# Scaling w_down by gb on chip, one VectorE step per output piece, and a last tile in finer pieces

## The chip, the cores and the metric

The kernel runs on one core of a Trainium2 chip. The metric is the device time of one execution in microseconds (us). A profile shows the span from the first to the last instruction; the time is 1.9 to 2.0 us longer than the span. TensorE (PE; its weight loads are listed as PEld) multiplies matrices and accumulates in PSUM, of which the kernel uses eight banks; VectorE (DVE) and ScalarE (ACT) read the banks out; SyncEngine (SP) issues most of the loads and all stores of the result; POOL is GpSimd.

## The reference, cut to what matters

```python
x = x + ga * A(layernorm(x) * (1 + ca) + sa)       # linear attention block, gives x1
h = layernorm(x) * (1 + cb) + sb
x = x + gb * (( silu(h @ w_gate) * (h @ w_up) ) @ w_down)
```

S = 2048 rows, D = 1024, F = 3584. `gb` is a row of 1024 numbers computed from the condition `c` and `w_mod`. Because `gb` multiplies columns of the product, `gb * (g @ w_down)` equals `g @ (w_down * gb)`: the factor can be applied to the weights once, instead of to every output.

## The kernel before

The rows are worked in four chunks of 512. After the attention part, gate/up (GU) of a chunk makes 28 blocks of `silu(gate) * up`, and the output stage (D) multiplies them with `w_down`, which GU of chunk 1 has loaded into SBUF. The order is GU0, GU1, D0, GU2, D1, GU3, D2, D3. Five banks rotate in `nextbank`.

```python
def gu_mm(sc_, f):                       # one block of gate and up
    g_ps = nextbank()                    # 8 matmuls of 512 columns
    ...
    nc.scalar.activation(out=sg[:], in_=g_ps[:], func=ACT.Silu)
    u_ps = nextbank()                    # 8 matmuls of 512 columns
    ...
    nc.vector.tensor_tensor(out=gus[sc_][:, f, :], in0=u_ps[:], in1=sg[:], op=ALU.mult)   # L537

def d_mm(st, h, cols=None):              # one piece of an output tile of 128 rows
    ...
    y_ps = nextbank()
    for f in range(FC):                  # FC = 28
        nc.tensor.matmul(y_ps[:, 0:w], lhsT=gus[sc_][:, f, t * P:(t + 1) * P], rhs=wd(f)[:, c0:c1], ...)  # L554
    yt = yts[h % 2]
    ob = obs[st % 2]
    nc.vector.tensor_tensor(out=yt[:, 0:w], in0=y_ps[:, 0:w], in1=gb_bc[:, c0:c1], op=ALU.mult)           # L558
    nc.vector.tensor_tensor(out=ob[:, c0:c1], in0=yt[:, 0:w], in1=x1rs[st % 2][:, c0:c1], op=ALU.add)     # L559
    nc.sync.dma_start(out=out2[st * P:(st + 1) * P, c0:c1], in_=ob[:, c0:c1])                             # L560
```

Each tile of 128 rows is made in two pieces of 512 columns; the last tile (tile 15) in 512, 256 and 256.

## Time and profile before

842.83 us, the median of 3 runs (842.6 to 843.38). These are lines of the profile's page: the span, the busy time of each engine, and the shares of the chain of work that ended last.

```profile
span 840.4 us, 10575 instructions
...
PE 827.8 (99%) x4182; PEld 390.6 (46%) x4264; DVE 361.5 (43%) x672; ACT 145.1 (17%) x271; POOL 79.8 (10%) x143
...
PE 97%; SPq 1%; DMA 1%; issue 1%; DVE 0%
```

PE is the engine that everything waits for. The view of the waits, cut to what PE waited for (total us, times, longest), says how little it stands still:

```profile
PE bank L350 <- ACT M L222: 2.0, 3, 1.4
PE bank L195 <- DVE M L169: 1.2, 1, 1.2
PE bank L250 <- DVE M L232: 0.6, 2, 0.4
PE bank L365 <- DMA M<-in_w_mod_dram: 0.5, 1, 0.5
PE bank L250 <- DVE saT L370: 0.3, 1, 0.3
```

All five lines belong to the opening: neither gate/up (L529, L535) nor the output stage (L554) is in the list. The chain of waits from 826 us on shows the one place where VectorE is on the chain (columns: start us, us, what):

```profile
825.88 11.04 PE bank L554 x78
836.92 0.02 issue
836.95 0.43 DVE M L558
837.38 0.02 issue
837.40 0.42 DVE M L559
```

The groups of instructions by shape (count | busy us, mean ns | idle before and what ended it) give the durations for the costing:

```profile
L559 DVE TENSOR_TENSOR M<-M 128x512 bf16<-128x512 f32 x31 | 21.4, 692 | 1.1
L558 DVE TENSOR_TENSOR M<-bank,gb_bc 128x512 f32<-128x512 f32 x31 | 21.4, 692 | 145.4 <-PE bank L554 145.4
...
L639 DVE TENSOR_TENSOR M<-M,ga_bc 128x1024 bf16<-128x1024 bf16 x8 | 5.5, 682 | 0.0
...
L558 DVE TENSOR_TENSOR M<-bank,gb_bc 128x256 f32<-128x256 f32 x2 | 0.8, 424 | 3.8 <-PE bank L554 3.8
```

In D VectorE idles 145 us waiting for PE: a step taken away there is not time taken away. Two windows (stretch, its length, then busy us and count of each engine, granted clock, DMA share, GB/s): GU of chunk 1, and the first output stage.

```profile
353.00:450.00 97.00, 96.53 (x442) 44.02 (x450) 31.79 (x48) 17.89 (x30) 0.00 (x0) 1.00 0.78 238
450.00:498.00 48.00, 47.79 (x220) 21.72 (x223) 10.38 (x15) 0.00 (x0) 0.00 (x0) 1.00 0.23 73
```

VectorE is the third busy figure: 31.79 of 97 us, and 10.38 of 48.

### The profile page before, as it was taken

The numbers are of one execution on the slowest core, as the hardware profiler recorded it, in microseconds if no ns is written. First come the engines' busy times: TensorE is split into PE (matmuls) and PEld (weight loads), VectorE is DVE, ScalarE is ACT, GpSimd is POOL, SyncE is SP. The second block draws the span as 40 slices with busy tenths as digits, with TensorE's granted clock in tenths as the row PEclk, the third lists the DMA queues.
The fourth block names the chain that finished last, engine by engine and source line by source line (L and its number), as shares of the span: only waits on it lengthen the run. The fifth ranks groups of instructions, "written<-read, shape, count | busy, mean of one in ns | idle before, by whom it ended". The sixth has DMA issues, their size and how long they took to land.

```text
span 840.4 us, 10575 instructions
## 1 busy us (share of the span) xinstructions
PE 827.8 (99%) x4182; PEld 390.6 (46%) x4264; DVE 361.5 (43%) x672; ACT 145.1 (17%) x271; POOL 79.8 (10%) x143
## 2 busy tenths in 40 slices
PE   7999999999999999999999999999999999999998
PEld 4454554544444444444444444444444444444444
DVE  5768779988655655354111221111212111112222
ACT  4333333313211111111110001111000111100000
POOL 2124220022122323100000000000000000000000
PEclk9999999999999999999999999999999999999999
DMA  9985491055588899987874225555322555211220
GB/s 291 310 244 141 130 242 47 18 152 132 127 224 225 225 208 267 228 250 225 250 239 144 76 69 151 151 151 152 103 76 85 155 156 151 75 32 51 76 69 26
DMA packets 203761, 128.62 MB, mean 153 GB/s; under 512 B 50496, under 2 KB 189888, under 8 KB 203712
## 3 DMA queue, kind: packets, MB, share of 16 engines
q1 hardware_dynamic: 162864, 98.58, 40.9%
q10 hardware_dynamic: 38544, 20.98, 11.3%
q0 software_dynamic: 2304, 8.39, 2.6%
q8 instruction: 33, 0.54, 0.3%
q14 instruction: 16, 0.13, 0.0%
HBM read 103.81 MB, written 12.58 MB: 139 GB/s over the span
## 4 chain that ended last, share of the span: by engine, by line
PE 97%; SPq 1%; DMA 1%; issue 1%; DVE 0%
PE bank L554 23%; PE bank L535 23%; PE bank L529 23%; PE bank L486 7%; PE bank L265 7%; PE bank L273 7%; PE bank L250 6%; DMA M<-in_w_mod_dram 1%; PE bank L459 1%; PE bank L282 1%; SPq L149 1%; SPq L146 0%; PE bank L343 0%; PE bank L329 0%; SPq L141 0%
## 5 line engine op out<-in xcount | busy, mean ns | idle before, releaser
L535 PE MATMUL bank<-M,M 128*128 128x512 bf16 x880 | 210.2, 379 | 0.8
L529 PE MATMUL bank<-M,M 128*128 128x512 bf16 x875 | 209.9, 379 | 1.1
L537 DVE TENSOR_TENSOR M<-bank,e 128x512 bf16<-128x512 f32 x112 | 77.5, 692 | 262.5 <-PE bank L535 250.3
L554 PE MATMUL bank<-M,M 128*128 128x512 bf16 (+1 forms) x689 | 147.3, 370 | 0.7
L532 ACT ACTIVATE e<-bank 128x512 f32<-128x512 f32 x112 | 66.8, 597 | 436.2 <-PE bank L529 399.6
L554 PEld LDWEIGHTS <-M 128*128 128x128 bf16 x924 | 90.4, 98 | 103.3
L535 PEld LDWEIGHTS <-M 128*128 128x128 bf16 x896 | 87.7, 98 | 105.7
L529 PEld LDWEIGHTS <-M 128*128 128x128 bf16 x896 | 87.4, 98 | 103.8
L558 DVE TENSOR_TENSOR M<-bank,gb_bc 128x512 f32<-128x512 f32 (+1 forms) x33 | 22.3, 675 | 149.2 <-PE bank L554 149.2
L250 PE MATMUL bank<-M,M 128*128 128x512 bf16 x245 | 56.7, 379 | 1.5 <-DVE M L232 0.6
L486 PE MATMUL bank<-M,M 128*128 128x512 bf16 x252 | 57.6, 379 | 0.2
L273 PE MATMUL bank<-M,M 128*128 128x512 bf16 x247 | 57.0, 379 | 0.5
L265 PE MATMUL bank<-M,M 128*128 128x512 bf16 x252 | 55.7, 379 | 0.2
L245 ACT ACTIVATE e<-bank 128x512 f32<-128x512 f32 x64 | 37.8, 598 | 100.2 <-PE bank L273 48.8
L554 PE MATMUL bank<-M 128*128 128x512 bf16 x218 | 50.3, 379 | 0.2
L247 DVE SCALAR_TENSOR_TENSOR M<-bank,e 128x512 bf16<-128x512 f32 x64 | 44.3, 691 | 3.9
L265 PEld LDWEIGHTS <-M 128*128 128x128 bf16 x256 | 25.1, 98 | 30.2
L486 PEld LDWEIGHTS <-M 128*128 128x128 bf16 x256 | 25.0, 98 | 29.7
L250 PEld LDWEIGHTS <-M 128*128 128x128 bf16 x256 | 24.2, 98 | 29.5 <-DVE M L232 2.1
L246 DVE TENSOR_SCALAR e<-e 128x512 f32<-128x512 f32 x64 | 27.7, 433 | 23.2 <-ACT e L245 23.2
L273 PEld LDWEIGHTS <-M 128*128 128x128 bf16 x256 | 24.6, 98 | 27.6
L488 DVE TENSOR_TENSOR M<-bank,M 128x512 f32<-128x512 f32 x32 | 22.0, 689 | 14.6 <-PE bank L486 13.4
(74 smaller groups left out, 364.9 us busy)
## 6 DMA issues: line engine op xcount, KB each, us to landing
M<-in_B_w_gate_dram SPq DMA_DIRECT2D x56, 512.0 KB, 4.0
M<-in_B_w_up_dram SPq DMA_DIRECT2D x56, 512.0 KB, 5.0
M<-in_w_mod_dram SPq DMA_DIRECT2D x8, 1024.0 KB, 8.6
x_scratch<-M POOLq DMA_DIRECT2D x16, 512.0 KB, 5.9
M<-x_scratch ACTq DMA_DIRECT2D x16, 512.0 KB, 3.4
M<-in_B_w_down_dram SPq DMA_DIRECT2D x6, 1024.0 KB, 7.9
M<-in_A_x_dram SPq DMA_DIRECT2D x16, 256.0 KB, 6.5
M<-in_w_mod_dram SPq DMA_DIRECT2D x8, 512.0 KB, 7.0
```

Source lines behind the costliest of these rows:

```text
L245: nc.scalar.activation(out=e[:], in_=acc, func=ACT.Exp)
L246: nc.vector.tensor_scalar(out=e[:], in0=e[:], scalar1=1.0, scalar2=PHI_EPS, op0=ALU.min, op1=ALU.add)
L247: nc.vector.scalar_tensor_tensor(out=dst, in0=acc, scalar=0.0, in1=e[:], op0=ALU.max, op1=ALU.add)
L250: nc.tensor.matmul(acc[:], lhsT=M4[:, sc_, cc, t * P:(t + 1) * P], rhs=wk[:, cc, h * NB:(h + 1) * NB], start=(cc == 0), stop=(cc == DC - 1))
L265: nc.tensor.matmul(acc[:], lhsT=M4[:, sc_, cc, t * P:(t + 1) * P], rhs=wv[:, cc, h * NB:(h + 1) * NB], start=(cc == 0), stop=(cc == DC - 1))
L273: nc.tensor.matmul(acc[:], lhsT=wq[:, cc, qc * P:(qc + 1) * P], rhs=M4[:, sc_, cc, :], start=(cc == 0), stop=(cc == DC - 1))
L486: nc.tensor.matmul(acc[:], lhsT=oTs[st % 3][:, cc, :], rhs=wo[:, cc, hs], start=(cc == 0), stop=(cc == DC - 1))
L529: nc.tensor.matmul(g_ps[:], lhsT=wg_blk[:, cc, fs], rhs=M4[:, sc_, cc, :], start=(cc == 0), stop=(cc == DC - 1))
L532: nc.scalar.activation(out=sg[:], in_=g_ps[:], func=ACT.Silu)
L535: nc.tensor.matmul(u_ps[:], lhsT=wu_blk[:, cc, fs], rhs=M4[:, sc_, cc, :], start=(cc == 0), stop=(cc == DC - 1))
L537: nc.vector.tensor_tensor(out=gus[sc_][:, f, :], in0=u_ps[:], in1=sg[:], op=ALU.mult)
L554: nc.tensor.matmul(y_ps[:, 0:w], lhsT=gus[sc_][:, f, t * P:(t + 1) * P], rhs=wd(f)[:, c0:c1], start=(f == 0), stop=(f == FC - 1))
```

## The change

Its intent: apply `gb` to `w_down` while VectorE has room in GU of chunk 1, so that an output piece needs only one step (add x1, read straight from PSUM), and make the last piece of the last tile narrower, so that less work stands behind the last matmul. The computation of `gb` is moved forward from GU1 to GU0 and the start of GU1, since it is now needed earlier. The diff, cut:

```diff
-        yt = yts[h % 2]
         ob = obs[st % 2]
-        nc.vector.tensor_tensor(out=yt[:, 0:w], in0=y_ps[:, 0:w], in1=gb_bc[:, c0:c1], op=ALU.mult)
-        nc.vector.tensor_tensor(out=ob[:, c0:c1], in0=yt[:, 0:w], in1=x1rs[st % 2][:, c0:c1], op=ALU.add)
+        nc.vector.tensor_tensor(out=ob[:, c0:c1], in0=y_ps[:, 0:w], in1=x1rs[st % 2][:, c0:c1], op=ALU.add)
 ...
                 if st == ST - 1:
-                    add(("D", st, 1), lambda st=st: d_mm(st, 1, (NB, NB + NB // 2)))
-                    add(("D", st, 2), lambda st=st: d_mm(st, 0, (NB + NB // 2, D)))
+                    for i, c_ in enumerate(((512, 768), (768, 896), (896, 1024))):
+                        add(("D", st, 1 + i), lambda st=st, c_=c_: d_mm(st, 1, c_))
 ...
-    put(("GU", 0, 20), lambda: load_late(GB, 0, 0), lambda: load_late(GB, 1, 1))
+    put(("GU", 0, 18), lambda: load_late(GB, 0, 0), lambda: load_late(GB, 1, 1))
+    gb_at = [("GU", 0, f) for f in range(21, FC)] + [("GU", 1, f) for f in range(8)]
 ... (the sums, the split and the broadcast of gb follow gb_at)
+    for i in range(8):
+        for k, f in enumerate(wd_f[i]):
+            put(("GU", 1, max(3 * i + 4, 7 + i) + k // 2) if i < 7 else ("GU", 1, FC - 2 + k),
+                lambda f=f: nc.vector.tensor_tensor(out=wd(f), in0=wd(f), in1=gb_bc[:], op=ALU.mult))
```

More of the change, by code (lines that the diff above doesn't have):

```diff
@@ L120 @@
     obs = [view(M6, 4096 + 1024 * i, [D]) for i in range(2)]
-    yts = [view(M6, 6144 + 1024 * i, [NB], F32) for i in range(2)]
     accA = view(M5, 8256, [D], F32)
@@ L631 @@
     put(("Q", 1, 2), lambda: late_cols(SB, 0, hlA[0]), lambda: late_cols(SB, 1, hlA[1]), lambda: late_fin(SB))
-    put(("GU", 0, 20), lambda: load_late(GB, 0, 0), lambda: load_late(GB, 1, 1))
+    put(("GU", 0, 18), lambda: load_late(GB, 0, 0), lambda: load_late(GB, 1, 1))
+    gb_at = [("GU", 0, f) for f in range(21, FC)] + [("GU", 1, f) for f in range(8)]
     for kb in range(2):
-        sums(accG, kb, kb, [("GU", 1, 5 * kb + i) for i in range(4)])
-        put(("GU", 1, 5 * kb + 4), lambda kb=kb: late_split(accG, kb, hlG))
-        put(("GU", 1, 5 * kb + 6), lambda kb=kb: late_bc(kb, hlG, gb_bc))
+        sums(accG, kb, kb, gb_at[5 * kb:5 * kb + 4])
+        put(gb_at[5 * kb + 3], lambda kb=kb: late_split(accG, kb, hlG))
+        put(gb_at[5 * kb + 5], lambda kb=kb: late_bc(kb, hlG, gb_bc))
     for cc in range(DC):
@@ L679 @@
         put(("GU", 1, 3 * i + 1), lambda i=i: load_wd(i))
-    order = [(st, 0) for st in range(ST)]
+    wd_f = {i: range(4 * i, 4 * i + 4) if i < 3 else range(12, 14) if i == 3 else
+            range(14 + 4 * (i - 4), min(18 + 4 * (i - 4), FC)) for i in range(8)}
+    for i in range(8):
+        for k, f in enumerate(wd_f[i]):
+            put(("GU", 1, max(3 * i + 4, 7 + i) + k // 2) if i < 7 else ("GU", 1, FC - 2 + k),
+                lambda f=f: nc.vector.tensor_tensor(out=wd(f), in0=wd(f), in1=gb_bc[:], op=ALU.mult))
     put(("GU", 1, FC - 4), lambda: load_x1r(0), lambda: load_x1r(1))
```

## The prediction

What it works out from a page's figure (the 1.5 and 1.4 us at 81 ns per matmul) is an estimate.

> **What bounds the kernel now.** TensorE. It is busy (page) 827.8 of 840.4 us, the granted clock full in every slice; the chain that ended last is 97% PE. The view of the waits finds only 4.6 us of PE waiting for another engine, all in the opening; none in gate/up (GU) or the output stage (D). In D VectorE (DVE) is 22% busy; 149.2 us of its idle time ends on PE bank L554. So VectorE work in D is off the chain, except after the very last matmul: there the chain shows PE until 836.92, multiply L558 0.43, add L559 0.42, then the 64 KB store (1.6 us to landing), span 840.4.
>
> **What the change removes.** 33 multiplies at L558 (22.3 us of VectorE). Only the last (0.45 us with hand-over) is on the chain.
>
> **What it adds.** 28 multiplies of 128x1024 bf16. The same form scaling wo (L639) took 682 ns: 19 us more VectorE work in GU of chunk 1, where it is busy 31.8 of 97 us. (The Trainium skill, "VectorE: DVE Perf Modes", "What auto-detection actually checks", lets tensor_tensor reach a packed mode for 16-bit data; the trace agrees: 682 ns for 1024 bf16, 692 ns for 512 f32.) Does it stall PE?
> - Two bank fills last 3.45 us and five banks rotate, so an eviction may be some 6 us late before PE waits. Two multiplies behind one need 1.4 us; VectorE idles 2.76 us before each.
> - A multiply waits for its w_down load. Loads go out at 359.9, 366.8, 381.0, 387.9, 402.2, 409.1, 422.9, 429.8 and land 5.7 to 9.0 us later; the multiplies stand behind evictions at about 381, 384, 391, 402, 412, 423, 433, 447: 1 us or more of slack, then the banks' 6 us.
> - The last tile of w_down is scaled by about 451.6; D's first group reads it at about 456.
> - The gb loads go out at about 308 to 311 instead of 318.5, took 12 to 17 us, so land by about 328, when the first gb sum is due; 1 to 3 us late would not reach PE.
> So no new wait of PE.
>
> **The last tile.** Its last 256 columns become two groups of 128: 28 more matmuls. By the Trainium skill ("TensorE: Matmul & The Clock Gate", "Back-to-back issue gap") N=128 sustains 81 ns per matmul, which would cost 1.5 us here. This trace shows less: the sixteen 129-column matmuls of L282 start every 57 ns, the 256-column ones every 109. So 56 x 57 = 3.2 us against 28 x 109 = 3.05: +0.1 us. After the last matmul remains one add of 128 columns: 692 ns at 512 and 424 at 256 extrapolate to 0.29 us, against 0.89: -0.6 us. The 32 KB store should take 1.6 us, like 64 KB (1.6) and 128 KB (1.7).
>
> **Sum.** -0.5 us: 842.35 us, range 841.7 to 843.1. Chances: faster by over 2% 0.003, within 2% 0.99, slower 0.007.
>
> **What would show it.** VectorE busy falls about 3 us in total, rises in GU of chunk 1, halves in D; PE's waits stay in the opening; each 128-column group takes 1.6 us; 0.3 us between last matmul and store; span near 839.9.
>
> **What would make it wrong.** 128-column groups at 81 ns (+1.4 us); a multiply behind a late load holding PE (a PE wait at 350 to 455 us); the 32 KB store landing later; run-to-run spread (0.8 us before).

## The result, and the profile after

842.29 us, the median of 6 runs (842.0 to 842.52), beside 843.22 us for the kernel before (842.6 to 844.37, 6 runs). The ratio is 0.9988, with a 95% interval from 0.9975 to 1.0001: the same within 2%, and the interval reaches 1. (A ratio is the mean time of one kernel's fast runs over that of the other's of the same rounds, so not quite the ratio of the medians.) The lines of the page that answer to those of before:

```profile
span 840.4 us, 10723 instructions
...
PE 833.5 (99%) x4292; PEld 391.3 (47%) x4292; DVE 356.5 (42%) x668; ACT 145.1 (17%) x271; POOL 79.9 (10%) x143
...
PE 97%; SPq 1%; DMA 1%; issue 0%; DVE 0%
```

The span of this profile is that of the first profile of the kernel before, 840.4 us. (PE's busy time is higher partly because fewer matmul records are missing here: gate/up is recorded 2 x 896 times, against 880 and 875 before.) Line numbers moved: L553 is L554 of before, L556 is the one remaining step, L683 the scaling. What PE waited for:

```profile
PE bank L194 <- DVE M L168: 1.2, 1, 1.2
PE bank L349 <- ACT M L221: 0.8, 2, 0.5
PE bank L364 <- DMA M<-in_w_mod_dram: 0.8, 1, 0.8
PE bank L249 <- DVE M L231: 0.6, 2, 0.4
PE bank L249 <- DVE saT L369: 0.3, 1, 0.3
```

Again only the opening: the scaling made no wait of PE. The two windows:

```profile
353.00:450.00 97.00, 97.00 (x451) 43.99 (x450) 41.70 (x66) 17.30 (x29) 0.00 (x0) 1.00 0.78 238
450.00:498.00 48.00, 48.00 (x224) 21.76 (x223) 6.13 (x9) 0.00 (x0) 0.00 (x0) 1.00 0.23 73
```

VectorE went from 31.79 to 41.70 us in GU of chunk 1 and from 10.38 to 6.13 in the output stage. The groups, and the chain from 826 us on:

```profile
L556 DVE TENSOR_TENSOR M<-bank,M 128x512 bf16<-128x512 f32 x31 | 21.5, 692 | 165.1 <-PE bank L553 165.1
...
L683 DVE TENSOR_TENSOR M<-M,gb_bc 128x1024 bf16<-128x1024 bf16 x28 | 18.0, 683 | 0.0
...
L556 DVE TENSOR_TENSOR M<-bank,M 128x128 bf16<-128x128 f32 x2 | 0.6, 291 | 2.4 <-PE bank L553 2.4
```

```profile
825.86 11.38 PE bank L553 x108
837.24 0.02 issue
837.26 0.29 DVE M L556
```

Behind the last matmul stand 0.29 us of VectorE instead of 0.43 + 0.42. Yet the span is the same. To see why, the execution is cut into four parts, by three events that every kernel here has: the start of the first eviction of V (the end of the opening), the start of VectorE's step for the last 512-column piece (after it only the narrow pieces follow), and the landing of the last store.

| profile | opening | middle | last pieces, to the landing | closing, to the end of the span | span |
|---|---|---|---|---|---|
| before | 33.59 | 797.24 | 8.64 | 0.90 | 840.37 |
| after | 33.83 | 797.24 | 7.95 | 1.34 | 840.36 |

The middle, 95% of the execution with all of the scaling in it, is equal to 0.01 us. The last pieces gained 0.69 us. Of that, 0.44 us was given back in the closing, and 0.24 us was lost in the opening, which the change does not touch. The closing is read from SyncEngine's records (start and end in us, what it waits for; 100, 102, 104, 105, 107, 108, 109 and 110 are the eight semaphores that loads and stores use in turn, signalled when one has landed). The kernel before, store on semaphore 110 landed at 839.470:

```
837.855 838.187  issue of the last store, semaphore 110
838.233 838.250  wait 117
838.291 838.319  wait 118, 116
838.358 838.386  wait 100, 115
   ... six more waits, one every 0.06 us (102, 104, 105, 107, 108, 109) ...
839.487 839.515  wait 110, 106          <- the last store; nothing after it
840.368          end of the span
```

The changed kernel, store on semaphore 100 landed at 839.022:

```
837.577 837.909  issue of the last store, semaphore 100
837.955 837.983  wait 118, 117
839.038 839.066  wait 100, 116          <- the last store; seven more waits follow
839.105 839.133  wait 102, 115
   ... five more waits, one every 0.06 us (104, 105, 107, 108, 109) ...
839.472 839.500  wait 110, 106
840.358          end of the span
```

SyncEngine closes the program by waiting for the eight semaphores in a fixed order. In the kernel before the last store happened to use the last of them, so all other waits passed while the store was still under way. The added piece is one store more; the rotation moved on by one, the last store fell on the first semaphore, and the seven that follow were looked at only after the landing.

### The profile page after: what moved, and what is told of

The parts are those of the page before. It is cut to its first block, busy times and chain, and to the rows that moved or that the text cites. A ratio compares the mean times of both kernels' runs of the same rounds, so it can differ in the third digit from the quotient of the medians.

```text
span 840.4 us, 10723 instructions
## 1 busy us (share of the span) xinstructions
PE 833.5 (99%) x4292; PEld 391.3 (47%) x4292; DVE 356.5 (42%) x668; ACT 145.1 (17%) x271; POOL 79.9 (10%) x143
## 4 chain that ended last, share of the span: by engine, by line
PE 97%; SPq 1%; DMA 1%; issue 0%; DVE 0%
PE bank L553 23%; PE bank L534 23%; PE bank L528 23%; PE bank L272 7%; PE bank L485 7%; PE bank L264 7%; PE bank L249 6%; DMA M<-in_w_mod_dram 1%; PE bank L458 1%; PE bank L281 1%; SPq L148 1%; SPq L145 0%; PE bank L342 0%; SPq L140 0%; PE bank L328 0%; PE bank L364 0%
## 5 line engine op out<-in xcount | busy, mean ns | idle before, releaser
L553 PE MATMUL bank<-M,M 128*128 128x512 bf16 (+2 forms) x728 | 148.0, 363 | 0.0
L553 PEld LDWEIGHTS <-M 128*128 128x128 bf16 x952 | 90.9, 98 | 103.0
L556 DVE TENSOR_TENSOR M<-bank,M 128x512 bf16<-128x512 f32 (+2 forms) x34 | 22.5, 661 | 169.9 <-PE bank L553 169.9
L553 PE MATMUL bank<-M 128*128 128x512 bf16 x224 | 51.0, 379 | 0.0
```

## The experiments

Theory: the gain is only what stands behind the last matmul (0.69 us), and the order of the closing waits gives 0.44 us of it back; the rest of what the times show is the opening's own spread. Rivals: the change gains or loses something in the body (less VectorE work in D, or the scaling holding PE up); or the closing waits don't matter. The first six below, up to the repeat, were timed in 5 rounds. By their times each of the six is the same within 2% as the kernel before, with an interval of the ratio that includes 1; what they decide, they decide in the traces.

### The last store back on the last semaphore

```diff
+        if st == ST - 2 and c0 == 0:
+            return
+        s0 = 0 if st == ST - 2 else c0
-        nc.sync.dma_start(out=out2[st * P:(st + 1) * P, c0:c1], in_=ob[:, c0:c1])
+        nc.sync.dma_start(out=out2[st * P:(st + 1) * P, s0:c1], in_=ob[:, s0:c1])
```

> The changed kernel with the two output stores of the last tile but one merged into one, so that the last store of all lands on the semaphore that the closing waits look at last, as in the kernel before. Theory (the gain at the end was given back by the closing waits): from the start of the eviction of the last 512-column group to the end of the span 8.85 us (7.95 to the landing, 0.90 after it), against 9.28 in the changed kernel and 9.54 in the kernel before; time about 0.4 us under the changed kernel. Rival (the closing waits don't matter, the change's gain comes from less VectorE work in the body): 9.28 us, time as the changed kernel. In both the distance between evictions in the body stays as before.

Measured: last pieces 8.00, closing 0.91: 8.91 us in all, 0.06 from the 8.85 of the theory and far from the 9.28 of the rival. Middle 797.25. The time did not show it: median 842.25 us (5 runs, 842.09 to 843.88), against 842.29 and 842.44 for the two series of the changed kernel. In this profile the opening took 34.21 us, 0.38 more than in the changed kernel's first profile, which hides it. The mechanism is confirmed in the trace; the expected 0.4 us in the time was a miss, and the opening's spread is as large.

### The kernel before, its last store on the first semaphore

```diff
+        for s0, s1 in ([(0, 256), (256, 512)] if st == ST - 2 and c0 == 0 else [(c0, c1)]):
+            nc.sync.dma_start(out=out2[st * P:(st + 1) * P, s0:s1], in_=ob[:, s0:s1])
-        nc.sync.dma_start(out=out2[st * P:(st + 1) * P, c0:c1], in_=ob[:, c0:c1])
```

> The kernel before with one store of the last tile but one split in two, so that the last store moves to the first of the eight store semaphores; no compute is touched. Theory: landing unchanged (8.64 us after the start of the last 512-column eviction), but 1.34 us instead of 0.90 from the landing to the end of the span, so about 0.4 us slower than the kernel before. Rival: no difference at all, 9.54 us.

Measured: last pieces 8.56, closing 1.32. Splitting one store of an earlier tile, without touching any compute, made the closing 0.42 us longer. The landing was expected unchanged, but came 0.08 us earlier. So the net cost of the move is 0.34 us here (9.88 against 9.54), and 0.38 in the changed kernel (9.29 against 8.91 with the store moved back). The store's own time goes with this: on the last semaphore of the order a last store took 1.60 to 1.62 us from the start of its issue to the landing with 64 KB and 1.50 with 32 KB, on the first 1.53 and 1.45 to 1.46 (32 KB on the fifth, in a run below: 1.45). Why was not followed up. Median 843.42 us against 842.9 for the kernel before (9 runs). The interval of the ratio (0.9993 to 1.0018) does not exclude 1; the trace does show the step.

### The scaling alone

```diff
-                    for i, c_ in enumerate(((512, 768), (768, 896), (896, 1024))):
+                    for i, c_ in enumerate(((512, 768), (768, 1024))):
```

(against the changed kernel)

> The scaling of w_down and the single VectorE step, but the last tile ends in pieces of 512, 256, 256 as in the kernel before (same number of stores, so the last one keeps its semaphore). Theory: only the multiply at the very end goes, 0.46 us: landing 8.18 us after the start of the last 512-column eviction, 0.90 after it, 9.08 in all against 9.54 before and 9.28 in the full change: this half alone beats the full change by 0.2 us. Rival (gain in the body): the same as the full change from the body, span differing in its middle.

Measured: last pieces 8.18, closing 0.90: 9.08 us, as expected to 0.01. The scaling with its single step is worth 0.46 us, and this half keeps it all. Median 842.24 us; two of the five runs were at 844.2, at a mean clock of 0.998 (see below).

### The finer pieces alone

```diff
-                    add(("D", st, 1), lambda st=st: d_mm(st, 1, (NB, NB + NB // 2)))
-                    add(("D", st, 2), lambda st=st: d_mm(st, 0, (NB + NB // 2, D)))
+                    for i, c_ in enumerate(((512, 768), (768, 896), (896, 1024))):
+                        add(("D", st, 1 + i), lambda st=st, i=i, c_=c_: d_mm(st, 1 + i, c_))
```

(against the kernel before)

> The kernel before, multiply and add in the output stage, only the last tile's end in pieces of 512, 256, 128, 128. Theory: two steps of 0.29 us instead of two of 0.42 (-0.27), matmuls +0.06, the smaller store -0.17: landing 8.26 us after the start of the last 512-column eviction, then 1.34 us since the added store moves the last one to the first semaphore: 9.60 against 9.54, no gain or a loss of 0.06 us. Rival (smaller pieces help by themselves): 9.16 us, a gain of 0.4.

Measured: last pieces 8.28, closing 1.32: 9.60 us against 9.54 before. The finer pieces alone gain 0.36 us up to the landing and lose 0.42 after it. Median 843.12 us.

This profile also fell on one of the longer runs (843.61 us), and shows where it was longer. The opening took 34.87 us. The view of the waits has a line that the other profiles lack:

```profile
PE bank L250 <- DMA M<-in_A_wqkv_dram: 0.7, 1, 0.7
```

And in the table of windows the stretch of 15 to 20 us has a granted clock (the figure before the last two) of 0.80:

```profile
15.00:20.00 5.00, 4.76 (x47) 2.13 (x46) 2.08 (x8) 0.00 (x0) 0.00 (x0) 0.80 1.08 319
```

The clock's records put it at half from 13.62 to 17.03 us, 3.41 us, which costs at most 1.7 us of PE's work. The last wait before it was the 0.74 us for that load, and the longest the 1.2 us at the very start of the span. In the runs of all kernels but the control below (862.35 us), every run above 844 us whose clock was listed had a mean granted clock of 0.997 or 0.998 (some faster runs list 0.998 as well).

### Two pieces instead of three

```diff
-                    for i, c_ in enumerate(((512, 768), (768, 896), (896, 1024))):
+                    for i, c_ in enumerate(((512, 896), (896, 1024))):
```

(against the changed kernel)

> The changed kernel, but the last tile ends in pieces of 512, 384, 128 columns: as narrow a last piece with one store less, so the last store keeps the semaphore of the kernel before. Theory (tail and closing waits): 8.91 us from the start of the eviction of the last 512-column group to the end of the span (8.00 to the landing, 0.90 after it), as in the run with the merged store and against 9.28 in the changed kernel. First eviction of V to that eviction: 797.25 us as in all. Rival (the third piece is worth something by itself): longer than 8.95. The time's median depends on the opening, which spread over 1.3 us in the six profiles so far, so it may lie anywhere within 0.6 us of the changed kernel's.

Measured: last pieces 7.93, closing 0.91: 8.84 us, the shortest end of all, 0.70 us less than the kernel before and 0.45 less than the changed kernel. The third piece is worth nothing. The median is 842.30 us (6 runs, 841.95 to 844.34) against 842.74 for the kernel before; two of the six runs were longer ones with the lower clock, so the means give a ratio of 1.0 (0.9987 to 1.0012). This is the version that the experiments point to; its advantage is shown in the trace and not in the time.

### The change repeated

> The changed kernel once more, beside five fresh rounds of the kernel before. Theory: tail 9.28 us, body 797.25 us, so a true gain near 0.26 us; the measured gain of 0.9 us between the medians of the first comparison should shrink toward 0.3, and only the opening should differ from the first profile. Rival (the first comparison's 0.9 us was real, from the body): the gap between the medians stays near 0.9 us and the body is shorter.

Measured: median 842.44 us (5 runs, 842.22 to 842.6) against 842.74 us (11 runs, 842.28 to 844.48): 0.30 us between the medians, ratio 0.9993 (0.9981 to 1.0005). Last pieces 7.95, closing 1.33. The gap of 0.93 us between the medians of the first series shrank toward the 0.25 us that the end shows (other groups of runs are wider apart; see what stays open, below). One thing was not as expected: the middle was 797.60, 0.35 longer. Compared event by event with the other profiles, the difference has arisen by 123 us, in the attention part, which the change does not touch; from there on the spacing is the same. The second experiment had the same hitch at the same place, 0.20 us long. What causes it was not followed up.

### The scaling done twice

```diff
-                lambda f=f: nc.vector.tensor_tensor(out=wd(f), in0=wd(f), in1=gb_bc[:], op=ALU.mult))
+                lambda f=f: [nc.vector.tensor_tensor(out=wd(f), in0=wd(f), in1=m, op=ALU.mult)
+                             for m in (gb_bc[:], ones_bc)])
```

(against the changed kernel, with a tile of ones set in time; one look)

> The changed kernel with each row block of w_down multiplied a second time, by ones (28 more multiplies of 0.68 us; result unchanged). Theory (VectorE has room in gate/up of chunk 1): VectorE busy there from 41.7 to about 61 us of 97, no PE wait after the opening, body 797.25 us. Rival (the scaling costs PE something): body longer, by some of 19 us, and PE waits between 380 and 460 us.

Measured: VectorE busy 60.14 us of the 97 (the third busy figure below), PE's waits only in the opening, middle 797.25 us.

```profile
353.00:450.00 97.00, 97.00 (x451) 43.99 (x450) 60.14 (x94) 17.30 (x29) 0.00 (x0) 1.00 0.78 239
```
Doubling the cost in dispute changed nothing; the rival falls.

### The scaling done four times

The same edit with `for m in (gb_bc[:], ones_bc, ones_bc, ones_bc)`; one look, as a control that a delay of VectorE would be seen at all.

> A control: each row block of w_down multiplied four times (once by gb, three times by ones; result unchanged), 57 us more VectorE work than the changed kernel, which had 55 us of it free in gate/up of chunk 1. Theory (an eviction may be some 6 us late before PE waits): VectorE is full there, evictions fall behind by more than 6 us, and PE waits in all some 5 to 12 us between 390 and 470 us, for VectorE. If PE does not wait at all, the estimate of the room was too small; if it waits much more than 12 us, the five banks give less than 6 us.

Measured: 862.35 us; the middle was 816.83, 19.6 us longer. PE waited 15.1 us for VectorE, more than the 5 to 12 expected. The line of the waits, and the stretch of 395 to 405 us with its granted clock of 0.66:

```profile
PE bank L528 <- DVE M L536: 15.1, 6, 5.0
395.00:405.00 10.00, 5.02 (x14) 1.77 (x13) 9.66 (x15) 0.60 (x1) 0.00 (x0) 0.66 0.35 103
```

The timeline of VectorE and of PE around the first of these waits (start us, us, then in brackets the idle time before it):

```profile
388.56 0.68 DVE L685 TENSOR_TENSOR M<-M,gb_bc 128x1024 bf16<-128x1024 bf16 x1
...
399.67 0.68 DVE L536 TENSOR_TENSOR M<-bank,e 128x512 bf16<-128x512 f32 x1
...
386.63 1.89 PE L534 MATMUL bank<-M,M 128*128 128x512 bf16 x8
...
393.54 1.89 PE L534 MATMUL bank<-M,M 128*128 128x512 bf16 x7
400.41 3.57 PE L528 MATMUL bank<-M,M 128*128 128x512 bf16 x8 [4.98 <-DVE M L536]
```

The group of matmuls that ended near 388.5 was evicted at 399.67, 11.2 us late; PE ran on until about 395.4 and then stood for 4.98 us. So an eviction could be about 11.2 - 5.0 = 6.2 us late before PE waited: the estimate of some 6 us from five banks holds. The wait was longer than expected, it seems, because the room was counted over all of GU1, while the multiplies only begin at 382 us: 16.7 us of the 55 lie before that (in the changed kernel VectorE is busy 12.3 of the 29 us from 353 to 382). Most of the remaining 4.5 us goes with the granted clock, which was at half from 397.79 to 404.62 and from 466.06 to 469.47 us: PE worked in 7.6 us of this, which costs some 3.8 us by estimate. Some 0.7 us is not accounted for.

### The whole last tile in pieces of 128

```diff
+                if st == ST - 1:
+                    for i in range(8):
+                        add(("D", st, i), lambda st=st, i=i: d_mm(st, 1, (128 * i, 128 * i + 128)))
```

(in place of the 512, 256, 128, 128 of the changed kernel; one look)

(The page meant below is the Trainium skill's "TensorE: Matmul & The Clock Gate", section "Back-to-back issue gap"; the 19.9 us are an estimate from its figure.)

> The changed kernel with the whole last tile in eight groups of 128 columns: 224 matmuls of 128 columns in a row. If they follow each other every 55.7 ns as the 56 of the changed kernel did, the tile takes 12.5 us instead of 12.2, and from the start of the eviction of the last 512-column group (now that of the tile before) to the landing of the last store it is about 14.25 us (13.99 in the changed kernel, measured from the same eviction). If the 81 ns of the Trainium skill's tensor engine page hold for a long run, 19.9 us. The last store moves four semaphores on, to the fifth of eight: by the theory of the closing waits 1.09 us from landing to the end of the span, between 0.90 (last) and 1.33 (first); by the rival that only the first is special, 0.90.

Measured: 14.27 us to the landing, where 14.25 was expected for 55.7 ns per matmul and 19.9 for 81 ns. VectorE's steps, each set off by the end of a group of 28 matmuls, begin 1.56 us apart, which is 55.8 ns per matmul:

```profile
834.32 0.29 DVE L556 TENSOR_TENSOR M<-bank,M 128x128 bf16<-128x128 f32 x1 [1.27 <-PE bank L553]
835.88 0.29 DVE L556 TENSOR_TENSOR M<-bank,M 128x128 bf16<-128x128 f32 x1 [1.27 <-PE bank L553]
```

The closing was 1.09 us: the last store used the fifth of the eight semaphores, and three more waits followed it. With 0.90 for the last and 1.33 for the first, the closing grows by about 0.06 us for each wait that stands behind the last store.

### The kernel before, three more profiles

> The unchanged kernel before, profiled again (first of three), to see where its runs differ from one another: its 23 runs without a drop of the granted clock lie between 842.28 and 843.75 us, those of the changed kernel between 842.00 and 842.60. Theory: tail 9.54 us (start of the eviction of the last 512-column group to the end of the span), first eviction of V to that eviction 797.25 us, at most 0.35 longer by a hitch in the first stage; all the rest of the spread is in the opening, before the first eviction of V (33.6 to 34.9 us so far). Rival: gate/up or the output stage of the kernel before takes longer in its slower runs, which the change cures; then the stretch from 215 us on is longer here than in the changed kernel.

> The unchanged kernel before, second of three profiles. Theory: tail 9.54 us and the stretch after the first stage as in the first profile to within 0.05 us, the spread in the opening. Rival: the stretch from 215 us on is longer in a slower run.

> The unchanged kernel before, third of three profiles. Theory: tail 9.54 us and the stretch after the first stage as in the first profile to within 0.05 us, the spread in the opening. Rival: the stretch from 215 us on is longer in a slower run.

Measured: openings 34.01, 34.20 and 34.10; middles 797.25, 797.24 and 797.25; last pieces 8.63 and closings 0.91 in all three; times 842.70, 842.88 and 842.78 us. Nearly all of the difference to the first profile (842.26 us, opening 33.59) is in the opening. The rival, slower stretches later on in the kernel before, finds no support in these profiles; but none of them fell on a run above 842.9 us, so the slower half of its runs was not seen. (That the 23 runs named above had no drop of the clock is not known for all: one, of 843.05 us, lists 0.998, and for the first six no clock is listed.)

All profiles by part, in us (in the narrow tile the last 512-column piece belongs to the tile before, so its two middle figures are not comparable with the others):

| profile | opening | middle | last pieces | closing | span |
|---|---|---|---|---|---|
| before | 33.59 | 797.24 | 8.64 | 0.90 | 840.37 |
| before, three more | 34.01, 34.20, 34.10 | 797.25, 797.24, 797.25 | 8.63 | 0.91 | 840.80, 840.99, 840.89 |
| before, store moved | 33.95 | 797.45 | 8.56 | 1.32 | 841.28 |
| pieces alone | 34.87 | 797.25 | 8.28 | 1.32 | 841.72 |
| scaling alone | 34.02 | 797.24 | 8.18 | 0.90 | 840.34 |
| after | 33.83 | 797.24 | 7.95 | 1.34 | 840.36 |
| after, repeated | 33.60 | 797.60 | 7.95 | 1.33 | 840.49 |
| after, store moved | 34.21 | 797.25 | 8.00 | 0.91 | 840.36 |
| two pieces | 34.08 | 797.25 | 7.93 | 0.91 | 840.16 |
| scaled twice | 34.00 | 797.25 | 7.96 | 1.34 | 840.54 |
| scaled four times | 34.20 | 816.83 | 7.95 | 1.34 | 860.32 |
| narrow last tile | 33.74 | 791.20 | 14.27 | 1.09 | 840.31 |

## Why the prediction was right or wrong

The predicted 842.35 us (841.7 to 843.1) met the 842.29 us measured, and "within 2%" was the outcome. That the number met so closely is luck: it was 0.5 us below the 842.83 us of the kernel before, which in the rounds of the comparison took 843.22, so that the medians lay 0.93 us apart, while the traces show a gain of 0.25. The reasons held in these points:

- **No new wait of PE.** The middle is equal to 0.01 us with the scaling, and with twice the scaling (but for the hitch in the repeat, which arose before the scaling begins). The room of some 6 us before a late eviction stops PE was confirmed at about 6.2 us by the control.
- **The only VectorE work on the chain is after the last matmul.** The scaling alone gained exactly that: 0.46 us at the end, nothing elsewhere, though it took a multiply out of all 33 output pieces.
- **128-column matmuls every 57 ns.** The trace's own 57 ns was the right guide, not the 81 ns of the skill's page: 56 ns in a run of 224. The three narrow groups took 0.06 us more than the two groups of before (0.1 predicted).
- **0.29 us for the last add** was measured as 0.29, and from the last matmul to the store 0.36 us including hand-overs, against 0.95 before.

What was mis-sized or missing:

- **The sum.** Up to the landing the gain was 0.69 us, not 0.5: 0.59 between last matmul and store, 0.17 because the last store landed in 1.45 us instead of 1.61 (1.6 had been predicted), less 0.06 for the matmuls. Of the 0.17, some 0.05 goes with the move to the first semaphore: 32 KB on the last one took 1.50.
- **The closing was not in the sum.** "Span near 839.9" came from 840.4 - 0.5 and took the time after the landing as constant. The added store moved the last one to the first of eight semaphores, and 0.44 us came back in the closing (0.38 net of the earlier landing). The gain that the end of the kernel shows is therefore 9.54 - 9.28 = about 0.25 us, half of the prediction.
- **The opening.** It was named only as run-to-run spread. In the profiles it differs by 0.6 us, and by 1.3 us with the profile that has the clock drop, two to five times the gain that the end keeps; a range of 1.4 us was the right size.
- VectorE's busy time fell by 5.1 us rather than 3, mostly because each multiply overlaps the end of the instruction before it, another multiply or an eviction: the 28 take 18.0 us together, and add only 16.8 us to VectorE's busy time, not 19.

What stays open: the changed kernel's 11 runs have a median of 842.38 us, the 27 runs of the kernel before that were made by then one of 842.92 us. That gap of 0.54 us is twice the 0.25 us that the traces show. The openings don't explain it: leaving out the profile with the clock drop in the opening, they average 33.97 us in the five profiles of the kernel before and its variant, and 33.96 us in the eight of the changed kernel and its variants. The kernel before also had 4 of 27 runs above 844 us and the changed kernel none of 11; variants with the same scaling and opening had such runs, so chance may do it, but the runs do not settle it. Both intervals of the ratio reach 1. Nor did the runs show why the loads of the opening land earlier or later.

## What to carry to other kernels

When one engine is busy 97% of the chain, taking work off another is worth only what stands behind the last instruction of the first; here 0.46 us of 22 us removed. Size an end effect to the end of the span, not to the last store: in these kernels the number of loads and stores decides which semaphore the last store signals, and each closing wait behind it costs about 0.06 us, up to 0.44 us (0.34 to 0.38 net of the earlier landing). For differences of tenths of a us, cut the traces at events that all versions share; the times of whole runs, with an opening that spreads by 0.6 to 1.3 us, cannot tell them apart.

## What the Trainium skill lacked or had wrong

- "TensorE: Matmul & The Clock Gate", section "Back-to-back issue gap": it gives 81 ns per matmul as the sustained rate at N=128, with the isolated gap of about 56 ns under-counting. Here 224 matmuls of 128 columns, each with its own weight load, followed each other every 56 ns; the isolated formula was right for a long run. For N=512 it gives 131 ns sustained and calls about 216 ns an over-count; here a 512-column group of 28 took 6.04 us, 216 ns each. This is said of that section alone, not of the whole page.
- The same page, "Part 1: The HAM clock gate", names at least one idle window of about 3.4 us as the cause of the half clock. In one run the clock fell to half for 3.41 us in the opening although no single wait of PE before it was longer than 1.2 us (the last two were 0.48 and 0.74 us, on either side of a group of eight 128-column matmuls). In the control it fell for 6.83 us when PE had stood still for 2.36 us (in the wait of 4.98 us), and for 3.41 us about 1.1 us after a wait of 2.39 us had ended, while waits of 2.54 and 2.76 us between them made no drop. The length of the drop agrees with the page; in these three cases PE had not been idle for a whole window of that length when the clock fell.
- No page that was consulted tells of the closing waits of SyncEngine over the eight load-and-store semaphores, nor that the position of the last store's semaphore in that order moves the end: 0.90 us from landing to end with it last, 1.09 with three waits behind it, 1.32 to 1.34 with it first.
